# One load of ten weight rows issued as two, and waits left out that others imply, in a decode step of attention and MLP

## The chip, the cores and the metric

The kernel runs on one core of a Trainium2 chip, in one launch. The metric is the device time of one execution in microseconds (us): the kernel before takes 401.53 us, the median of 3 runs that lie between 401.38 and 401.64.

## The reference

One token passes through grouped-query attention over a cache of 65,536 positions and through a mixer with an MLP; both branches read the same normalised input and are added to it.

```python
def _A_ref(x, k_cache, v_cache, wq, wo):          # Hq = 32, Hkv = 4, Sk = 65536, Dh = 128
    q = (x @ wq).reshape(B, Sq, Hq, Dh)           # transposed to heads
    scores = jnp.einsum("bhqd,bhkd->bhqk", q, k) * (Dh ** -0.5)
    p = _softmax(scores, axis=-1)
    o = jnp.einsum("bhqk,bhkd->bhqd", p, v)
    return o.reshape(B, Sq, Hq * Dh) @ wo         # 4096 -> 1024

def _B_ref(x, w1, w2, w3, w4):                    # D = 1024, F = 3584
    h = _gelu(_layernorm(x) @ w1)
    hs = concatenate([g0, g1, g2, g3]) @ w2       # quarters of h, shifted by 1 or 2 tokens
    x1 = x + hs
    return x1 + _gelu(_layernorm(x1) @ w3) @ w4   # 3584 -> 1024

xn = _layernorm(A_x)
out = A_x + _A_ref(xn, ...) + _B_ref(xn, ...)
```

All inputs are bf16. K and V caches are 64 MB each and the weights are 42 MB together: some 170 MB are read for one row of 1,024 numbers. With one token the shifted quarters are all zero; the kernel keeps them as a tile of zeros and still multiplies it with w2.

## The kernel before, in words

**Staging.** One SBUF tile, KV, holds all large data: two slots for K (KOFF), two for V (VOFF). K comes in 16 loads of 4 MB and V in 8 loads of 8 MB; a load is issued as soon as the readers of its slot are done. All of them, and all weights, are issued by SP (`load_rows` L320, `issue_k` L334, `issue_v` L342), so they share one hardware queue, whose transfers are spread over 16 DMA engines: 8 of the 128 partitions for each engine. Every load has a semaphore of its own channel, which the 16 engines together raise by 16.

**The main loop.** There are 32 steps n, 8 for each of the 4 KV heads, each over 8,192 positions. A step transposes K on DVE (L494), forms the scores on PE (QK, L504), takes a shared bound from row maxima (stats1, MB, stats2; L511 to L521), exponentiates on ACT (L532), transposes the result through PE and DVE (L540, L542), multiplies with V on PE (PV, L550) and adds to an accumulator on POOL (FLASH, L558 to L563). Steps are written once and emitted as a loop on PE, ACT, POOL and DVE (`emit_looped`, L68): only one turn's instructions are stored, and the values of waits are computed from the turn's number (L96). SP's work isn't looped.

**The order of the work.** It is written by hand. A small planner adds the waits: each engine has a queue `_Q` with one counting semaphore, each buffer `_B` remembers which events wrote it (`w`) and read it (`r`). `_deps` (L118) makes an operation wait for the writers of what it reads and for writers and readers of what it writes. `_Q.wait` (L25) leaves a wait out when the same engine has already waited for as much on that semaphore since the last mark; each wait that is left is an instruction of its own on its engine. A full write (`set_write`) forgets earlier writers and readers, a partial one (`add_write`) does not.

**The end.** While the last steps run, SP issues w1, w2 and w3 into slots that have come free (L622 to L625), after the last step wo and the first 16 rows of w4 (L627, L628), and, when PE has read w1 and w2, the rest of w4 into their place (L652 to L658). A "row" here is 256 KB: 128 partitions with 1,024 bf16 numbers each; wo has 32 such rows, w4 has 28. The order of the queue is thus w1, w2, w3, wo, w4 rows 0 to 15, w4 rows 16 to 25, w4 rows 26 and 27.

PE's last work is, in this order: the product with w3, whose result goes through gelu into `gh_bf`; the 32 rows of wo (`half_rows`, L666); w4's first 16 rows; a small addition of the wo result into the output (L694); w4's ten rows; w4's two rows. `out_rows` (L449 to L456) does a part of w4: each row is four matmuls (L453), one for each quarter of 256 output columns, on four column groups of PE, all accumulated in the PSUM tile OUT_ps. Before each part PE waits for that part's load:

```python
w4_parts = [(0, 16, KOFF[1], b_K[1][0]), (16, 10, KOFF[0], _B()), (26, 2, KOFF[0] + 10 * D, _B())]
...
out_rows(*w4_rows(1))
out_rows(*w4_rows(2), last=True)
_op(q_dve, lambda e: e.tensor_copy(orow, OUT_ps[:, 0:256]), reads=[b_OUT], writes=[b_p[0]])
```

DVE then copies OUT_ps to bf16 (L700), SP stores 2 KB (L701) and waits for the store.

Of the kernel before, what the change touches and what calls it, by code (L numbers as in the profile page):

```python
# [13 lines left out]
class _Q:  # L14
    def __init__(self, name, sem, in_order=False):
        self.name = name
        self.sem = sem
        self.in_order = in_order
        self.ops = []
        self.cnt = 0  # L20
        self.waited = {}
        self.marks = []
        self.var = None
# [76 lines left out]
class _B:  # L100

    def __init__(self, name=""):
        self.name = name
        self.w = {}
        self.r = {}

    def set_write(self, ev):
        self.w = {ev[0]: ev[1]}
        self.r = {}

    def add_write(self, ev):
        self.w[ev[0]] = max(self.w.get(ev[0], 0), ev[1])

    def add_read(self, ev):
# [1 line left out]


def _deps(q, reads, writes):  # L118
    for b in reads:
        for s, v in b.w.items():  # L120
            q.wait((s, v))
    for b in writes:
        for s, v in list(b.w.items()) + list(b.r.items()):
            if not (q.in_order and s is q.sem):
                q.wait((s, v))


def _done(ev, reads, writes, partial=False):
# [9 lines left out]
def _op(q, fn, reads=(), writes=(), partial=False, tick=True):  # L138
    _deps(q, reads, writes)
    ev = q.op(fn, tick)  # L140
    _done(ev, reads, writes, partial)
    return ev


def _grp(q, fns, reads=(), writes=(), partial=False):
    _deps(q, reads, writes)
    ev = None
    for i, fn in enumerate(fns):
        ev = q.op(fn, i == len(fns) - 1)
    _done(ev, reads, writes, partial)  # L150
    return ev
# [8 lines left out]
def _dma(q, chan, fn, reads=(), writes=(), partial=False):  # L160
    _deps(q, reads, writes)
    chan.n += 1
    ev = q.dma(fn, chan.sem, 16 * chan.n)
    _done(ev, reads, writes, partial)
    return ev


def bass_parallel_sum__gqa_block_cached__mixer_s_mlp__decode_kernel(
# [14 lines left out]
    D = A_x.shape[2]  # L183
# [17 lines left out]
    with ExitStack() as es:  # L201
# [57 lines left out]
        KOFF, VOFF = (0, 16384), (32768, 65536)  # L259
# [39 lines left out]
        b_K = [[_B(), _B()], [_B(), _B()]]  # L299
# [149 lines left out]
        def out_rows(items, reads, last=False):  # L449
            fns = []  # L450
            for lhs, rhs in items:
                for jj in range(4):
                    fns.append(lambda e, lhs=lhs, rhs=rhs, jj=jj: e.matmul(  # L453
                        OUT_ps[32 * jj:32 * jj + 1, 0:256], lhs, rhs[:, 256 * jj:256 * jj + 256],
                        start=False, stop=last, tile_position=(0, 32 * jj), skip_group_check=True))
            _grp(q_pe, fns, reads=reads, writes=[b_OUT], partial=True)  # L456
# [192 lines left out]
        layer_norm(x1, b_x1, xn3, xn3_bf, b_xn3, 300)  # L649

        wo_sb = KV[:, VOFF[1]:VOFF[1] + 32 * D]
        w4_parts = [(0, 16, KOFF[1], b_K[1][0]), (16, 10, KOFF[0], _B()), (26, 2, KOFF[0] + 10 * D, _B())]  # L652
        for i, (r0, nr, c0, b_w) in enumerate(w4_parts):
            if i:
                for b in b_K[0]:
# [4 lines left out]
        def w4_rows(i):  # L660
            r0, nr, c0, b_w = w4_parts[i]
            return [(gh_bf[:, r:r + 1], KV[:, c0 + (r - r0) * D:c0 + (r - r0 + 1) * D]) for r in range(r0, r0 + nr)], [b_w, b_gh]
# [33 lines left out]
                                              start=False, stop=False, tile_position=(32 * (jj // 2), 32 * jj), skip_group_check=True)  # L696
                    for jj in range(4)], reads=b_ge + [b_const], writes=[b_OUT], partial=True)
        out_rows(*w4_rows(1))
        out_rows(*w4_rows(2), last=True)
        _op(q_dve, lambda e: e.tensor_copy(orow, OUT_ps[:, 0:256]), reads=[b_OUT], writes=[b_p[0]])  # L700
        ev_out = _dma(q_sp, chan("out"), lambda e: e.dma_start(out=out[0, 0, :].rearrange("(j n) -> j n", j=4), in_=orow[0:97:32, :]), reads=[b_p[0]])  # L701
        q_sp.wait(ev_out)
# [34 lines left out]
```

## Time and profile before

| what | us |
|---|---|
| median of 3 runs (lowest, highest) | 401.53 (401.38, 401.64) |
| the profiled execution | 401.81 |
| its span, from the first to the last instruction | 400.6 |
| busy: PE matmul, DVE, POOL, ACT | 167.6, 232.9, 91.8, 48.6 |
| DVE L494, transposes of K, 128 of 1.2 us | 149.5 |
| PE L504 and L550, scores and V | 60.4 and 58.6 |
| transfers of SP's queue | 169.87 MB, 98.3% of 16 engines' span |

The span is one execution, recorded by the hardware; the time of a run lies around it. Busy is the time in which an engine worked, idle the time before an instruction together with what ended it. A load is "landed" when all 16 engines have raised its semaphore. The granted clock is the share of PE's full clock that was let through.

### The profile page before, as it was taken

How to read it: one execution, taken by the hardware profiler on the slowest of the kernel's cores; microseconds unless marked ns; L12 is line 12 of the kernel's file. 1: busy time of each engine (PE TensorE's matmuls, PEld its weight loads, DVE VectorE, ACT ScalarE, POOL GpSimd, SP SyncE). 2: the span in 40 equal slices, each digit the busy share in tenths (PEclk: the TensorE clock that was granted, in tenths of full speed). 3: DMA queues.
4: the chain of work that ended last, by engine and by line, in shares of the span. 5: the costliest groups of instructions: out<-in, count | busy, mean ns of one | idle time of the engine just before them, and what ended most of it. 6: DMA issues, size and time to landing. Idle time of an engine off the chain costs nothing.

```text
span 400.6 us, 4647 instructions
## 1 busy us (share of the span) xinstructions
PE 167.6 (42%) x1488; PEld 54.5 (14%) x1504; DVE 232.9 (58%) x399; ACT 48.6 (12%) x132; POOL 91.8 (23%) x173
## 2 busy tenths in 40 slices
PE   0044233445243525352534364145335443455494
PEld 0022110111011101010111111011101110122232
DVE  0024756784688288738864886587667756643300
ACT  1000010111021101110111020111111110110000
POOL 6000013232135212230253031314232222250000
PEclk9997556555556656555555556656555555565886
DMA  9989999999999999899999998999999999999894
GB/s 393 439 373 471 414 416 422 484 398 422 458 440 406 422 474 445 389 425 468 425 409 445 474 425 386 455 442 425 429 438 461 419 422 404 474 434 459 381 425 179
DMA packets 4768, 169.98 MB, mean 424 GB/s; under 512 B 660, under 2 KB 664, under 8 KB 792
## 3 DMA queue, kind: packets, MB, share of 16 engines
q1 hardware_dynamic: 4616, 169.87, 98.3%
q8 instruction: 5, 0.08, 0.1%
q10 hardware_dynamic: 144, 0.00, 0.0%
q14 instruction: 3, 0.02, 0.0%
HBM read 169.87 MB, written 0.00 MB: 424 GB/s over the span
## 4 chain that ended last, share of the span: by engine, by line
DMA 56%; DVE 21%; PE 12%; issue 9%; another core or an unknown queue 1%; DVEq 0%; POOL 0%; ACT 0%; SPq 0%; ACTq 0%; POOLq 0%
DMA KV<-in_A_k_cache_dram 41%; DVE KV L494 16%; DMA KV<-in_B_w_dram 10%; PE S_ps L504 9%; DMA x_bf<-in_A_x_dram 6%; DVE mrow L511 2%; PE OT_ps L550 1%; PE MM_ps L465 1%; PE OUT_ps L453 1%; DVE pT_f L542 1%; PE MB_ps L517 1%; DVE Bst L521 0%; DVE Rm L512 0%; DVE brun L530 0%
## 5 line engine op out<-in xcount | busy, mean ns | idle before, releaser
L494 DVE STREAM_TRANSPOSE KV<-KV 128x1024 f32<-128x1024 f32 x128 | 149.5, 1211 | 21.8 <-DMA KV<-in_A_k_cache_dram 21.8
L504 PE MATMUL S_ps<-KV,Ycur 128*32 128x512 bf16 x512 | 60.4, 620 | 98.9 <-DVE KV L494 98.6
L550 PE MATMUL OT_ps<-KV,pT_f 128*32 128x512 bf16 x512 | 58.6, 608 | 35.2 <-DVE pT_f L542 34.4
L563 POOL TENSOR_TENSOR O_acc<-O_acc,tmpO 128x513 f32<-128x513 f32 x32 | 40.9, 1277 | 122.6 <-ACT tmpO L558 122.6
L511 DVE TENSOR_REDUCE mrow<-S_ps 128x1 f32<-128x512 f32 x32 | 22.1, 692 | 39.8 <-PE S_ps L504 39.8
L532 ACT ACTIVATE p_sb<-S_ps,brun 128x512 bf16<-128x512 f32 x32 | 22.0, 686 | 135.6 <-DVE brun L530 118.7
L558 ACT ACTIVATE tmpO<-OT_ps 128x512 f32<-128x512 f32 x32 | 19.2, 599 | 139.4 <-PE OT_ps L550 80.3
L504 PEld LDWEIGHTS S_ps<-KV,Ycur 128*32 128x32 bf16 x512 | 14.5, 126 | 123.2 <-DVE KV L494 94.2
L542 DVE STREAM_TRANSPOSE pT_f<-PT_ps 128x512 f32<-128x512 f32 x32 | 22.8, 713 | 13.5 <-PE PT_ps L540 11.0
L560 POOL TENSOR_TENSOR spare<-ff 128x1 f32<-128x1 f32 x32 | 6.2, 194 | 100.8 <-ACT ff L536 98.9
L550 PEld LDWEIGHTS OT_ps<-KV,pT_f 128*32 128x32 bf16 x512 | 15.6, 130 | 51.1 <-DVE pT_f L542 29.3
L561 POOL TENSOR_SCALAR O_acc<-O_acc,ff 128x514 f32<-128x514 f32 x32 | 22.5, 703 | 0.2 <-issue 0.2
L540 PE MATMUL PT_ps<-p_sb,permR 128*128 128x512 bf16 x16 | 8.6, 540 | 22.0 <-ACT p_sb L532 22.0
L517 PE MATMUL MB_ps<-Rm,Lmat 128*128 128x16 bf16 x32 | 6.2, 193 | 25.6 <-DVE Rm L512 25.6
L521 DVE TENSOR_REDUCE Bst<-MB_ps 128x1 f32<-128x16 f32 x32 | 5.6, 175 | 14.2 <-PE MB_ps L517 14.2
L382 PE MATMUL MM_ps<-ln_s,ones_f 128*128 128x1 f32 x6 | 1.8, 362 | 27.3 <-DVE ln_s L381 27.3
L378 DVE CAST xT<-x_bf 128x8 f32<-128x8 bf16 x1 | 0.2, 173 | 21.6 <-DMA x_bf<-in_A_x_dram 21.6
L666 PE MATMUL S_ps<-KV,o_bf 128*1 128x512 bf16 x64 | 8.8, 443 | 5.1 <-DMA KV<-in_A_wo_dram 5.1
L517 PEld LDWEIGHTS MB_ps<-Rm,Lmat 128*128 128x128 bf16 x32 | 3.3, 103 | 53.7 <-DVE Rm L512 53.7
L394 POOL TENSOR_TENSOR ln_s<-ln_s,neghalf 128x1 f32<-128x1 f32 x3 | 1.7, 560 | 37.0 <-DVE ln_s L392 37.0
L540 PEld LDWEIGHTS PT_ps<-p_sb,permR 128*128 128x128 bf16 x32 | 3.3, 102 | 47.9 <-ACT p_sb L532 47.9
L534 DVE TENSOR_TENSOR dd<-brun 128x1 f32<-128x1 f32 x32 | 5.4, 170 | 3.6
(112 smaller groups left out, 117.5 us busy)
## 6 DMA issues: line engine op xcount, KB each, us to landing
KV<-in_A_k_cache_dram SPq DMA_DIRECT2D x16, 4096.0 KB, 23.6
KV<-in_B_w_dram SPq DMA_DIRECT2D x1, 7168.0 KB, 33.0
KV<-in_B_w_dram SPq DMA_DIRECT2D x2, 2048.0 KB, 14.3
KV<-in_B_w_dram SPq DMA_DIRECT2D x1, 4096.0 KB, 34.9
KV<-in_B_w_dram SPq DMA_DIRECT2D x1, 2560.0 KB, 38.5
KV<-in_B_w_dram SPq DMA_DIRECT2D x1, 512.0 KB, 39.3
KV<-in_A_v_cache_dram SPq DMA_DIRECT2D x8, 35.9
x_bf<-in_A_x_dram ACTq DMA_DIRECT2D x1, 2.0 KB, 22.2
```

What stands on the lines that cost most here:

```text
L494: ev = q_dve.op(lambda e, c=c: e.transpose(out=KV32[:, c:c + 1024], in_=KV32[:, c:c + 1024]))
L504: fns.append(lambda e, we=we, cm=cm, mv=mv: e.matmul(S_ps[32 * cm:32 * cm + 32, :], Ycur[:, we, :, :].rearrange("p a g -> p (a g)"), mv, s ...
L511: _op(q_dve, lambda e: e.reduce_max(mrow[:, m:m + 1], S_ps[:, :], axis=AX.X), reads=[b_S], writes=[b_mrow[m]])
L517: _op(q_pe, lambda e: e.matmul(MB_ps[:, 0:16], Lmat[:, :], Rm[:, m, :], start=True, stop=True), reads=[b_R[m], b_const], writes=[b_MB])
L532: _op(q_act, lambda e: e.activation(p_sb[:, m, :], S_ps[:, :], ACTF.Exp, bias=brun[:, m:m + 1], scale=SCALE, accum_out=tmpO[:, cL:cL + 1]) ...
L540: _op(q_pe, lambda e: e.matmul(PT_ps[:, :], permR[:, :], p_sb[:, m, :], start=True, stop=True), reads=[b_p[m], b_const], writes=[b_PT])
L542: _op(q_dve, lambda e: e.transpose(out=pT_f[:, :], in_=PT_ps[:, :]), reads=[b_PT], writes=[b_pT])
L550: fns.append(lambda e, q=q, q4=q4: e.matmul(OT_ps[32 * q4:32 * q4 + 32, :], pT_bf[:, q, :, 1], KV[:, v0 + 512 * q:v0 + 512 * (q + 1)], sta ...
L558: _op(q_act, lambda e: e.activation(tmpO[:, 1:513], OT_ps[:, :], ACTF.Copy), reads=[b_OT], writes=[b_tmpO])
L561: b_Oacc.set_write(q_pool.op(lambda e: e.tensor_scalar(out=O_acc[:, :], in0=O_acc[:, :], scalar1=ff[:, m:m + 1], scalar2=0.0, op0=ALU.mult ...
L563: ev = q_pool.op(lambda e: e.tensor_tensor(out=O_acc[:, m:m + 513], in0=O_acc[:, m:m + 513], in1=tmpO[:, m:m + 513], op=ALU.add), tick=(s_ ...
L666: _grp(q_pe, [lambda e, lhs=lhs, rhs=rhs, jj=jj: e.matmul(S_ps[32 * jj:32 * jj + 1, :], lhs, rhs[:, 512 * jj:512 * jj + 512], start=False, ...
```

## The change

Two things are changed. The ten rows of w4 that follow the first sixteen are loaded as six and four, each with its own semaphore and buffer, and PE does them as two groups, each behind its own load. The places in SBUF, the order of rows and the last two rows' load are as before.

In `_deps`, waits are first gathered with the highest value for each semaphore and then issued, so an operation waits once for a semaphore where it could wait twice with a lower value first. And for a buffer whose last write was a full one and which has been read since, an operation that overwrites it waits for the readers only, since each reader has itself waited for that write. This holds for every engine, in the loops and outside.

```diff
@@ class _B
+        self.whole = False
     def set_write(self, ev):
         self.w = {ev[0]: ev[1]}
         self.r = {}
+        self.whole = True
     def add_write(self, ev):
+        self.whole = False
         self.w[ev[0]] = max(self.w.get(ev[0], 0), ev[1])
@@ def _deps(q, reads, writes):
+    need = {}
     for b in reads:
         for s, v in b.w.items():
-            q.wait((s, v))
+            need[s] = max(v, need.get(s, 0))
     for b in writes:
-        for s, v in list(b.w.items()) + list(b.r.items()):
+        for s, v in (list(b.r.items()) if b.r and b.whole else list(b.w.items()) + list(b.r.items())):
             if not (q.in_order and s is q.sem):
-                q.wait((s, v))
+                need[s] = max(v, need.get(s, 0))
+    for s, v in need.items():
+        q.wait((s, v))
@@ the end
-        w4_parts = [(0, 16, KOFF[1], b_K[1][0]), (16, 10, KOFF[0], _B()), (26, 2, KOFF[0] + 10 * D, _B())]
+        w4_parts = [(0, 16, KOFF[1], b_K[1][0]), (16, 6, KOFF[0], _B()), (22, 4, KOFF[0] + 6 * D, _B()), (26, 2, KOFF[0] + 10 * D, _B())]
...
         out_rows(*w4_rows(1))
-        out_rows(*w4_rows(2), last=True)
+        out_rows(*w4_rows(2))
+        out_rows(*w4_rows(3), last=True)
```

## The prediction

> **What bounds the kernel now.** I read the page first (engines, DMA row, queues), then the chain of waits near the end, then the windows of the last microseconds, then the timeline rows of the instructions that the change touches.
>
> The page, part 2 and part 3: the busy share of the 16 DMA engines in 40 slices of 10 us, and the queue that SP feeds.
>
> ```profile
> span 400.6 us, 4647 instructions
> ...
> DMA  9989999999999999899999998999999999999894
> ...
> q1 hardware_dynamic: 4616, 169.87, 98.3%
> ```
>
> The transfers of SP's queue fill 98.3% of the span; only the last slice (4 tenths) is not full. No engine is near that: DVE has 58%, PE 42%. So from about 2 us on, the span is 170 MB through full DMA engines, and a step counts only if it lies before the first or after the last of these bytes, or lets the queue run dry. The chain of waits, from 345 us (start, us, what):
>
> ```profile
> 357.10 38.50 DMA KV<-in_B_w_dram
> 395.59 0.04 issue
> 395.64 2.76 PE OUT_ps L453 x36
> 398.39 0.02 issue
> 398.42 0.42 DVE p_sb L700
> ```
>
> The piece of 38.50 us is the ten-row load of w4, issued at 357.10 behind everything still queued. It lands at 395.60, and only then do PE's last matmuls begin. After its landing the chain has 2.76 us of PE, 0.42 of DVE and the store. Three windows of the end (us, then PE, PEld, DVE, ACT, POOL busy with counts, granted PE clock, DMA share, GB/s):
>
> ```profile
> 390.00:394.00 4.00, 2.06 (x64) 1.16 (x56) 0.00 (x0) 0.00 (x0) 0.00 (x0) 0.99 0.98 417
> 394.00:396.00 2.00, 0.36 (x8) 0.24 (x12) 0.00 (x0) 0.00 (x0) 0.00 (x0) 0.50 0.45 176
> 396.00:397.00 1.00, 1.00 (x28) 0.69 (x20) 0.00 (x0) 0.00 (x0) 0.00 (x0) 0.50 0.04 16
> ```
>
> The DMA share falls from 0.98 to 0.45 to 0.04: the 16 engines run dry one after another over some 2 us, and the latest of them sets each landing. PE stands still from 392.06 (the end of the 391.45 row below) to 395.64, and its clock is 0.99 before and 0.50 after. PE's and SP's timeline rows, and the loads with their size and time from issue to landing:
>
> ```profile
> 389.60 1.92 PE L453 MATMUL OUT_ps<-KV,gh_bf 128*1 128x256 bf16 x64 [0.91 <-DMA KV<-in_B_w_dram]
> 391.45 0.61 PE L694 MATMUL OUT_ps<-KV,ones_f 1*1 1x256 f32 x8
> 395.64 2.73 PE L453 MATMUL OUT_ps<-KV,gh_bf 128*1 128x256 bf16 x48 [3.58 <-DMA KV<-in_B_w_dram]
> ```
>
> ```profile
> 354.65 0.36 SPq L320 DMA_DIRECT2D KV<-in_B_w_dram  x1
> 357.10 0.33 SPq L320 DMA_DIRECT2D KV<-in_B_w_dram  x1
> 357.47 0.43 SPq L320 DMA_DIRECT2D KV<-in_B_w_dram  x1
> ```
>
> ```profile
> KV<-in_B_w_dram SPq DMA_DIRECT2D x1, 4096.0 KB, 34.9
> KV<-in_B_w_dram SPq DMA_DIRECT2D x1, 2560.0 KB, 38.5
> KV<-in_B_w_dram SPq DMA_DIRECT2D x1, 512.0 KB, 39.3
> ```
>
> The three SP rows are the loads of 16, 10 and 2 rows; with the times to landing they land at 354.65 + 34.9 = 389.55, 357.10 + 38.5 = 395.60 and 357.47 + 39.3 = 396.77. The 48 matmuls of the last PE row are ten rows plus two, four matmuls a row.
>
> **The change part by part.**
>
> *The split, on SP.* One more DMA issue of 0.33 to 0.43 us. The two-row load, queued behind it on SP, is issued at about 357.9 instead of 357.47. It has 39.3 us to land and SP's next work is the store at 398.87, so this costs nothing; without that cover it would cost 0.4. The new load's waits are for the readers of w1 and w2, which the first piece has already waited for.
>
> *The split, in the DMA engines.* The bytes are the same; one more boundary between loads is passed. Ten rows take 395.60 - 389.55 = 6.05 us, 0.605 a row; two rows take 396.77 - 395.60 = 1.17, 0.585 a row. If each load cost a fixed f on top, 2r + f = 1.17 and 10r + f = 6.05 give f = -0.05, with the rounding of the landings (0.1 us) some 0.15 either way. The other end is a load with nothing queued ahead: the store, 2 KB, is issued at 398.87 and the span ends at 400.6, 1.7 us at most. So f lies between -0.2 and 1.7. I take 0.1, near the row of the same kind, a small load in a full queue. The Trainium skill, "DMA: Bandwidth & Descriptors", section "Anatomy of one DMA — SWDGE (gpsimd) path", fits about 2.0 us of fixed cost to every DMA, and most of it is the receipt after the last byte; it was measured on the other issue path. If a queue paid that for each load, the sum below would come out some 1.1 us over today's time; by the landings above, it overlaps with the next load's data.
>
> *The split, on PE.* The wait for ten rows becomes a wait for six, one for four and one for two. Six rows land four rows earlier: 395.60 - 4 x 0.605 = 393.2. The 12 rows took 2.73 us at clock 0.50; the longest matmul on this tile lasts 0.42, so a row is (2.73 - 0.42) / 11 = 0.21 us. At clock 0.99 to 1.00 the 16 rows took 1.92 with matmuls of 0.27: (1.92 - 0.27) / 15 = 0.11 a row. At the slow clock throughout:
> - six rows: 393.2 + 0.04 + 5 x 0.21 + 0.42 = 394.7, a microsecond before the next landing;
> - four rows: landing 395.60 + 0.1, + 0.04 + 3 x 0.21 + 0.42 = 396.8;
> - two rows: landing 396.77 + 0.1 = 396.87, + 0.04 + 0.21 + 0.42 = 397.54.
>
> Today PE ends at 398.39, so 0.85 us go. Next in line is the two-row load's landing; the four rows end only 0.1 before it, so a finer split would gain no more. If the clock is still 1.00, the two rows take 0.11 + 0.27 and PE ends at 397.29: 1.10 us go. Which clock holds is open: the row at 391.45 ends at 392.06, the six rows start 1.2 us later, where PE now stands for 3.58. The Trainium skill, "TensorE: Matmul & The Clock Gate", Part 1, describes a free-running window of about 3.4 us after which an idle array falls to half clock; by it the early six rows may hold the gate open, and the sum would be the 1.10. The 0.99 and 0.50 of the windows agree with two levels, and no row decides which one it will be.
>
> *DVE and the store.* L700 (0.42), the store's issue and its landing follow PE as before. Moved, not changed.
>
> *The pruned waits.* No wait is added but PE's for the new load. Behind the last landing stand three waits (PE on the load, L700 on PE, the store on L700); none has a double, so nothing goes there: the gaps are 0.04 and 0.02. In the loops, waits that others imply go, a wait being a sequencer step between instructions. The most this can free on DVE is the "issue" of a turn in the chain, 1.1 + 0.47 us, eight times over: 12.6 us of DVE. But group L494 shows 21.8 us of idle ended by the K loads: DVE already waits 2.7 us a turn for data, so it would wait longer for the same bytes. K loads are issued 23.6 us ahead of their landing (median) while 4 MB take 16 x 0.605 = 9.7, so the queue holds some 14 us of other work when one is added. Bounds: 0 from these rows; a gain would need a slice of the DMA row under 8 before the last, and there is none. I take 0. Without the cover, it would be a gain, not a loss.
>
> **Sum.** The profiled execution took 401.81 us: span 400.6 and 1.2 around it. Less 0.85 to 1.10, it gives 400.7 to 401.0. The median of the runs shown is 401.53, 0.28 under that execution, so against the runs: 400.43 to 400.68. I take 400.6.
>
> **Rivals.**
> 1. *The extra load costs what a lone one does* (slower). If the boundary stalls the queue as long as the store takes, 1.7 us, both last landings move by that: 401.53 - 0.85 - 0.1 (in the 0.85 already) + 1.7 = 402.3. It decides from f = 0.95 us on. The two-row load, a small one in the same place, speaks against it. 8%.
> 2. *A code packet moves to the latest engine.* The DMA view of 390 to 400 us has one packet of the instruction queue q8 (five of them make 0.08 MB, so 16 KB), 0.6% of 16 engines x 10 us = 0.96 us of one engine. With fewer instructions these packets fall elsewhere. On the latest engine one delays the last landing by up to 0.96: 401.5. Before, five such packets in the span and 16 engines; mostly it misses. 15%. The mirror: the latest engine is rid of one it has now, 399.7. 8%.
> 3. *It doesn't do what it says*: the six rows' last engine is so late, or PE's start of each part so slow, that PE still ends its rows in one run, and time stays at 401.5. The 2 us spread of the engines speaks for it; that each load's 16 parts follow in order on each engine, 0.6 us a row, against it. 14%.
>
> **How the numbers follow.** The forecast has 55%. A measurement here can tell about 0.2%, 0.8 us, from no change, and the forecast's low end (0.85) lies just beyond that, so I count 7 of its 55 as within. Faster: 48 + 8 = 56%; within 0.2%: 7 + 15 + 14 = 36%; slower: 8%. The range leaves out 402.3 and 399.7 (16% together): 400.2, half of the spread of the runs (0.26) and a little more under the 400.43, to 401.6.
>
> **What would show it.** After the change: PE on OUT_ps in three runs of 24, 16 and 8 matmuls, starting near 393.2, 395.7 and 396.9, each released by its own load; the idle of 3.58 us before the last run gone; L700 at about 397.3 to 397.6 instead of 398.42; the two-row load landing within 0.2 of 396.77; the DMA share of the span unchanged or higher. Wrong would be: the last landing at 397.8 or later (rivals 1 and 2), PE's last 24 matmuls in one run (rival 3), or a stretch of the loop in which the DMA share moved.

## The result, and the profile after

The changed kernel takes 400.68 us (median of 15 runs, 400.41 to 400.93), the kernel before beside it 401.55 (15 runs, 401.04 to 401.83): a ratio of 0.9979 with a 95% interval of 0.9972 to 0.9987, or 0.87 us less, between 0.5 and 1.1. The forecast was 400.6. The profiled execution of the changed kernel took 400.41 us, the lowest of its runs, that of before 401.81.

The page of the changed kernel, span and DMA row:

```profile
span 399.2 us, 4579 instructions
...
DMA  9989999999999999999999999999999999999995
```

The row is as full as before; 68 instructions fewer were recorded, and some 84 fewer ran, since the trace of before lacks 16 of PE's 1,504 matmuls. The end of the chain of waits (start, us, what; four pieces "issue" of up to 0.04 us left out):

```profile
356.89 0.33 SPq L327
357.26 0.43 SPq L327
357.74 38.81 DMA KV<-in_B_w_dram
396.55 0.04 issue
396.59 0.42 PE OUT_ps L460 x8
397.04 0.42 DVE p_sb L708
```

Before, the chain left the DMA at 395.59, with the ten rows' load, and 2.76 us of PE followed. Now it leaves it at 396.55, with the last load, and 0.42 us of PE follow. PE's three groups on the timeline (L460 is the old L453), and the times to landing of the last three loads:

```profile
392.96 0.83 PE L460 MATMUL OUT_ps<-KV,gh_bf 128*1 128x256 bf16 x24 [1.18 <-DMA KV<-in_B_w_dram]
395.39 0.61 PE L460 MATMUL OUT_ps<-KV,gh_bf 128*1 128x256 bf16 x16 [1.61 <-DMA KV<-in_B_w_dram]
396.59 0.39 PE L460 MATMUL OUT_ps<-KV,gh_bf 128*1 128x256 bf16 x8 [0.59 <-DMA KV<-in_B_w_dram]
```

```profile
KV<-in_B_w_dram SPq DMA_DIRECT2D x1, 1536.0 KB, 36.0
KV<-in_B_w_dram SPq DMA_DIRECT2D x1, 1024.0 KB, 38.1
KV<-in_B_w_dram SPq DMA_DIRECT2D x1, 512.0 KB, 38.8
```

The six, four and two rows are issued at 356.89, 357.26 and 357.74 and land at 392.89, 395.36 and, by the chain, 396.55. Each group waits for its own load and is done before the next one lands. The same windows as before (PE, PEld, DVE, ACT, POOL busy with counts, granted PE clock, DMA share, GB/s):

```profile
390.00:394.00 4.00, 2.60 (x80) 1.40 (x68) 0.00 (x0) 0.00 (x0) 0.00 (x0) 1.00 0.98 411
394.00:396.00 2.00, 0.60 (x16) 0.29 (x16) 0.00 (x0) 0.00 (x0) 0.00 (x0) 1.00 0.54 221
396.00:397.00 1.00, 0.39 (x9) 0.10 (x8) 0.00 (x0) 0.00 (x0) 0.00 (x0) 1.00 0.02 8
```

The clock is 1.00 to the end, where it was 0.50 before. From the last landing to PE's end it was 398.39 - 396.77 = 1.62 us before and is 397.01 - 396.55 = 0.46 now: 1.16 of the 1.40 us between the two profiled executions. The other 0.22 is an earlier landing, which w4's first load shows already (issued at 354.41, landed 34.9 us later, at 389.31 now; 389.55 before), so it is not the split's; in unsplit kernels PE starts on that load's rows between 389.22 and 389.73. The medians differ by 0.87 and not by 1.40 because the two profiled executions lie at opposite ends: that of before is 0.26 over the median of before, that of the changed kernel 0.27 under its own.

Two statements ahead of the prediction are to be corrected. The weights are some 36 million bytes, not 42 (170 read, less 134 for two caches of 64 times 2^20 bytes each). And not every wait is an instruction of its own: in the records most waits stand inside the instruction that needs them (353 such instructions on DVE before), and only some are a step by themselves (16 on DVE, 34 on SP).

### The profile page after: what moved, and what is told of

Same layout as the page of the kernel before. It is cut to its first block, busy times and chain, and to the rows that moved or that the text cites. A ratio compares the mean times of both kernels' runs of the same rounds, so it can differ in the third digit from the quotient of the medians.

```text
span 399.2 us, 4579 instructions
## 1 busy us (share of the span) xinstructions
PE 173.8 (44%) x1504; PEld 53.7 (13%) x1504; DVE 233.2 (58%) x399; ACT 48.8 (12%) x132; POOL 91.5 (23%) x173
## 4 chain that ended last, share of the span: by engine, by line
DMA 57%; DVE 18%; PE 13%; issue 10%; ACT 1%; another core or an unknown queue 1%; POOL 0%; DVEq 0%; SPq 0%; ACTq 0%; POOLq 0%
DMA KV<-in_A_k_cache_dram 42%; DVE KV L501 13%; DMA KV<-in_B_w_dram 10%; PE S_ps L511 9%; DMA x_bf<-in_A_x_dram 6%; DVE mrow L518 2%; PE PT_ps L547 2%; PE OT_ps L557 1%; PE MM_ps L472 1%; ACT p_sb L539 1%; DVE pT_f L549 1%; PE MB_ps L524 1%; DVE Rm L519 0%; DVE Bst L528 0%
## 5 line engine op out<-in xcount | busy, mean ns | idle before, releaser
L557 PE MATMUL OT_ps<-KV,pT_f 128*32 128x512 bf16 x512 | 57.1, 594 | 19.5 <-DVE pT_f L549 18.7
L547 PE MATMUL PT_ps<-p_sb,permR 128*128 128x512 bf16 x32 | 17.5, 547 | 44.3 <-ACT p_sb L539 44.3
## 6 DMA issues: line engine op xcount, KB each, us to landing
KV<-in_B_w_dram SPq DMA_DIRECT2D x1, 4096.0 KB, 34.9
```

What stands on the lines that cost most here:

```text
L547: _op(q_pe, lambda e: e.matmul(PT_ps[:, :], permR[:, :], p_sb[:, m, :], start=True, stop=True), reads=[b_p[m], b_const], writes=[b_PT])
L557: fns.append(lambda e, q=q, q4=q4: e.matmul(OT_ps[32 * q4:32 * q4 + 32, :], pT_bf[:, q, :, 1], KV[:, v0 + 512 * q:v0 + 512 * (q + 1)], sta ...
```

## The experiments

Two theories shared the facts. The landing theory: the end is the last landing and the rows that PE still has to do then. The clock theory: the twelve rows were late only because PE's clock had fallen to a half while it waited. A third, the wait theory, gave the gain to the pruned waits.

### The split alone

The new `w4_parts` and the fourth `out_rows`, with the old `_deps`.

> The split of the ten rows alone, with all the old waits. Landing theory (the end is the last landing plus the rows that PE still has to do then, two instead of most of twelve): 0.85 to 1.1 us under the kernel before, ratio 0.9973 to 0.9979, PE's last run 8 matmuls of 0.4 to 0.65 us. Wait theory (the pruned waits gave the gain): within 0.2 us of before.

Measured: 400.60 us against 401.59, ratio 0.9982 (0.9973 to 0.9990): as much as the whole change. The end of its chain:

```profile
396.63 0.62 PE OUT_ps L453 x8
```

Two of its windows, with the granted clock as the third figure from the end:

```profile
390.00:394.00 4.00, 2.64 (x80) 1.42 (x68) 0.00 (x0) 0.00 (x0) 0.00 (x0) 1.00 0.98 410
394.00:396.00 2.00, 0.57 (x12) 0.37 (x16) 0.00 (x0) 0.00 (x0) 0.00 (x0) 0.65 0.60 246
```

In this execution the clock had fallen again (0.65 from 394 to 396 us, 0.50 from 396 on), although the six rows had been worked on just before, so the two rows took 0.62 instead of 0.42 us. That is the prediction's case of the slow clock, with its number: 0.21 + 0.42 = 0.63. The gain is there at either clock.

### The pruned waits alone

The new `_B` and `_deps`, with ten rows in one load.

> The pruned waits alone, the ten rows in one load as before. Landing theory: within 0.2 us of before, ratio 0.9995 to 1.0005; the idle of DVE that K loads end in the transposes (21.8 us before, 23.7 in the changed kernel) is again higher than before, since DVE is freed only to wait longer. Wait theory: some 0.8 us under before.

Measured: 401.69 against 401.59, ratio 1.0004 (0.9995 to 1.0012). The wait theory falls. The transposes' group on its page (busy, mean ns | idle before, and what ended it):

```profile
L501 DVE STREAM_TRANSPOSE KV<-KV 128x1024 f32<-128x1024 f32 x128 | 149.5, 1211 | 24.2 <-DMA KV<-in_A_k_cache_dram 24.2
```

24.2 us of idle against 21.8 before. This number alone proves little: it is 22.6 with the split alone and all the old waits.

### Twelve rows in one load

```diff
-w4_parts = [(0, 16, ...), (16, 10, ...), (26, 2, ...)]
+w4_parts = [(0, 16, ...), (16, 12, ...)]
```

> The other way: the kernel before with the ten and the two rows in one load of twelve, old waits. Landing theory: all twelve rows start behind the last landing, near 396.7, and take 2.7 us at the half clock: PE ends near 399.5 instead of 398.4, 1.0 us over before, ratio 1.0025. If a load boundary in the queue cost much (rival 1 of the prediction, 1.7 us), one boundary fewer would give more than the late rows cost: 0.6 us under before.

Measured: 402.83 against 401.59, ratio 1.0038 (1.0025 to 1.0051; five runs), 1.2 us over. Its last group on PE:

```profile
396.46 2.73 PE L453 MATMUL OUT_ps<-KV,gh_bf 128*1 128x256 bf16 x48 [4.78 <-DMA KV<-in_B_w_dram]
```

All twelve rows follow the last landing, at the half clock. With the changed kernel, the kernel before and this one, 2, most of 12 and all 12 rows stand behind the last bytes, and the medians rise in that order.

### Twelve loads of one row

In the changed kernel, `w4_parts` has twelve entries of one row behind the first sixteen.

> The changed kernel with its last twelve rows in twelve loads of one row: nine boundaries more than six, four and two. By the prediction's f of 0.1 us a boundary the last landing moves by 0.9 us, and one row less behind it gives 0.1 to 0.2 back: 0.7 us over the changed kernel, near the kernel before (ratio 0.999 to 1.001). If a boundary cost nothing: 0.1 to 0.2 under the changed kernel. If it cost what the lone store takes (rival 1, 1.7 us): some 15 us over before.

Measured: 400.77 against 401.57, ratio 0.9980 (0.9971 to 0.9989): not to be told from the changed kernel, against the 0.7 us that I expected over it. Its chain's end, and three of SP's issues:

```profile
387.22 9.50 DMA KV<-in_B_w_dram
396.71 0.04 issue
396.76 0.31 PE OUT_ps L460 x4
```

```profile
359.61 4.71 SPq L327 DMA_DIRECT2D KV<-in_B_w_dram  x1
```

```profile
364.37 14.45 SPq L327 DMA_DIRECT2D KV<-in_B_w_dram  x1
```

The last landing comes 396.71 - 389.11 = 7.60 us after w4's first load, against 396.55 - 389.31 = 7.24 in the changed kernel: 0.36 us for nine boundaries, 0.04 each, by one execution of each kernel. Rival 1 of the prediction (1.7 us) is out. A row less behind the last landing gives 0.11 back (0.31 against 0.42). The SP rows come back below.

### The clock alone: extra matmuls, no split

Three kernels are the kernel before with matmuls of the same shape behind the small addition L694, written to CM_ps and read by nobody: 112, 32 and 64 of them.

```diff
+        _grp(q_pe, [lambda e, r=r, jj=jj: e.matmul(
+            CM_ps[32 * jj:32 * jj + 1, 0:256], gh_bf[:, r:r + 1], wo_sb[:, r * D + 256 * jj:r * D + 256 * jj + 256],
+            start=True, stop=True, tile_position=(0, 32 * jj), skip_group_check=True)
+            for r in range(28) for jj in range(4)], reads=[b_V[1], b_gh], writes=[b_CM])   # 8 and 16 rows in the others
         out_rows(*w4_rows(1))
```

112 extra matmuls:

> The kernel before with 112 extra matmuls of the same shape, whose result nobody reads, on PE while it would wait for the ten rows; nothing is split or pruned. The extra work takes 112 x 0.027 = 3.1 us, from 392.06 to some 395.3, before the landing at 395.6. Clock theory (the half clock of PE behind its idle of 3.58 us makes the twelve rows late): the granted clock stays at 1.00, twelve rows take 11 x 0.11 + 0.27 = 1.5 instead of 2.73 us, and since the two rows' load is there by 396.8, PE ends near 397.2: 1.1 to 1.2 us under before, as much as the split. If only the split counts (the rows are late because they start late): no more than 0.2 under before.

Measured: 401.96 against 401.59, ratio 1.0017 (1.0008 to 1.0026): slower. The chain:

```profile
392.18 1.95 PE CM_ps L698 x67
394.13 1.68 issue
395.81 1.47 PE CM_ps L698 x45
397.29 1.32 PE OUT_ps L453 x48
```

The extra work did not fit: after 67 matmuls PE stands still for 1.68 us and waits for nothing that the profile shows ("issue"); then the other 45 run when the ten rows have already landed, and push them to 397. Why PE stood still is open. That it waited for its code is a guess: in 390 to 400 us this execution has two packets of the instruction queue where before has one, but one falls between 393 and 394 us (0.93 us of one engine), the other between 396 and 397, when PE has long gone on; and the runs with 32 and 64 extra matmuls below have the additional packet too (six in the span, five before) without such an idle, though there PE waits for its load at that time. PE goes on at 395.81, just behind the landing of the ten rows (355.64 + 40.1 = 395.74), which may be chance. So this run decides nothing on the time, but its twelve rows, at a clock of 1.00, took 1.58 us instead of 2.73.

32 extra matmuls:

> The kernel before with only 32 extra matmuls (8 rows' worth, result not read) behind the small addition, so that PE reaches its wait for the ten rows at some 393.0 and does not run into code that isn't loaded yet. Clock theory: the granted clock stays at 1.00 past 395.6, the twelve rows take 1.5 to 1.6 us instead of 2.73 and PE ends near 397.2 without any split: 1.0 to 1.2 us under before. If the extra work does not hold the clock: 48 matmuls in 2.73 us as before and no gain. If PE again stands still for code in its last run, by an idle ended by issue, the gain is smaller by that idle.

Measured: 401.28 against 401.57, ratio 0.9995 (0.9986 to 1.0005), which is no verdict on a mean: of 12 executions six took 400.52 to 401.08 us and six 401.48 to 401.93. The profiled one, of 400.62 us, had the clock at 1.00:

```profile
395.59 1.60 PE L453 MATMUL OUT_ps<-KV,gh_bf 128*1 128x256 bf16 x48 [2.61 <-DMA KV<-in_B_w_dram]
```

The same 48 matmuls at 0.50 take 2.73, 1.13 us more; the two groups' medians, 400.72 and 401.73, are 1.0 apart.

64 extra matmuls:

> The kernel before, unsplit and with its old waits, with 64 extra matmuls (16 rows' worth, result not read) behind the small addition: PE works to some 393.9 and waits 1.7 us instead of 3.6. With 32 extra matmuls the executions fell into two groups, near 400.6 and near 401.7. Clock theory: the groups are the two clocks of the last twelve rows, and with 64 the full clock holds in nearly all: median 400.5 to 400.8, as low as the split, although nothing is split. If the split is needed for the gain: above 401.2, or still two groups of like size. If PE stands still for code behind the extra work: its last run starts late, by an idle ended by issue.

Measured: 400.60 us, ten of eleven executions between 400.43 and 400.96. In the profiled one the clock stays at 1.00:

```profile
395.37 1.71 PE L453 MATMUL OUT_ps<-KV,gh_bf 128*1 128x256 bf16 x48 [1.77 <-DMA KV<-in_B_w_dram]
```

The time of the split kernels, without a split. The ratio to before is only 0.9988 (0.9979 to 0.9998), because the kernel before took 401.22 in this set: six of its 15 executions lay between 400.60 and 401.00, nine between 401.21 and 401.86. So the kernel before seems to fall into the two groups too, in shares that vary: beside the changed kernel only two of its 15 executions lay under 401.2. That they are PE's two clocks is shown for the profiled executions: 0.50 at the end in those of 401.81 (before) and 401.73 (the pruned waits alone), 1.00 in 400.62 and 400.52 here. For the others it is argued from the times.

### The changed kernel with 28 extra matmuls

```diff
 out_rows(*w4_rows(1))
+_grp(q_pe, [... for r in range(7) for jj in range(4)], ..., writes=[b_CM])
 out_rows(*w4_rows(2))
```

> The changed kernel with 28 extra matmuls (result not read) between its groups of six and four rows. The clock then is 1.00 in every execution and the two rows take 0.4 us instead of 0.4 or 0.6: 0.1 to 0.25 us under the changed kernel, ratio to before 0.997 to 0.998. If the changed kernel already runs its last rows at the full clock nearly always: no difference to it.

Measured: 400.77 against 401.57, ratio 0.9980 (0.9971 to 0.9989), like the changed kernel. With two rows left, the clock is worth 0.2 us at most (0.62 against 0.42), which this measurement does not tell. No version here beats the changed kernel.

### Without the cover: six V loads left out

```diff
 def issue_v(j):
-    if j >= NV:
+    if j >= 2:
         return
```

Once in the kernel before and once in the changed one.

> The kernel before without the last six of the eight V loads (all steps multiply with the first two V blocks; the attention result is not the reference's): 50 MB fewer, so that the DMA engines no longer set the pace of the loop. Landing theory: 40 to 100 us under before, with DVE's idle for K loads gone from the transposes and the DMA share below 0.9 in the loop. If the loop's engines set the pace already: within 10 us of before.

> The changed kernel with the same six V loads left out. Here the cover of the pruned waits is gone. If the prediction's statement holds (waits cost something, but lie beside the transfers), this is 0.8 us (the split at the end) plus 1 to 12 us (waits in eight turns of the loop) under the same cut of the kernel before. If the pruned waits cost nothing at all even without cover: 0.8 us under it or less.

Measured: 381.10 us (ratio to the kernel before 0.9493, 0.9477 to 0.9509) and 380.22 (0.9472, 0.9456 to 0.9488). Neither theory's number for the first came true: it is only 20 us under before. Between 60 and 320 us the DMA share is 0.66, 1.01 before, and DVE is busy 191 of 260 us: the loop's own engines now set its pace, not far below that of the transfers. DVE's idle for K loads in the transposes is 4.1 us with the old waits, where it was 21.8. The two windows (before, then the kernel before without the six loads; columns as above):

```profile
60.00:320.00 260.00, 110.94 (x905) 30.69 (x918) 180.26 (x271) 38.47 (x109) 69.65 (x115) 0.54 1.01 435
60.00:320.00 260.00, 125.54 (x985) 33.05 (x985) 191.29 (x287) 41.91 (x117) 74.12 (x121) 0.57 0.66 274
```

The cover is some 20 us thick. The transposes of K in the two, first and last start:

```profile
L494 DVE STREAM_TRANSPOSE KV<-KV x128: 1200/1203/1246, 42.7 to 325.3; 128x1024 f32<-128x1024 f32 x128
```

```profile
L501 DVE STREAM_TRANSPOSE KV<-KV x128: 1200/1202/1245, 41.0 to 324.5; 128x1024 f32<-128x1024 f32 x128
```

282.6 us with the old waits, 283.5 with the pruned ones: the loop isn't faster where nothing hides it. The 0.88 us between the two medians (four runs each) fits what the split gives at the end: PE ends 0.6 us after the last landing in the changed kernel, 1.5 in the other.

## Why the prediction was right

**The bound.** The DMA engines full from 2 to 394 us, with only the end to be shortened: borne out (DMA share 1.00 in that stretch, before and after). The gain lies between the last landing and PE's end.

**The split on PE.** Six rows were put at 393.2, four at 395.7, two at 396.87; they landed at 392.89, 395.36 and 396.55, each some 0.3 early, 0.24 of which was there before the split. With the two rows at 0.38 us (full clock) or 0.63 (half), the measured ones are 0.42 and 0.62. The two cases of 0.85 and 1.10 us stand in the traces as split alone (0.62) and changed kernel (0.42). Two of the signs were missed by little: the last landing is 0.22 from 396.77, where 0.2 was allowed, and L700's copy starts at 397.04, ahead of the 397.3 to 397.6. The range of 400.2 to 401.6 held no gain at all as well, so it is the three groups on the timeline and not the number that bear the account out.

**The clock, weighed and left open.** That was as far as the trace of before went, but one step was missing: in the last rows of the kernel *before* the clock was taken as fixed at a half. By the times of its runs it is not. Some lie near those that end at the full clock, though no profile of such a run of this kernel was kept. At the full clock the twelve rows end about as early as the two (397.22 us with 32 extra matmuls, 397.01 in the changed kernel). Hence a second way to the whole gain, more work on PE, which the prediction's own numbers (12 rows at 0.11 us) would have priced. It also lowers the median of before, and with it the gain, where many of its executions end early: 401.22 beside the 64 extra matmuls, 401.55 beside the changed kernel.

The Trainium skill, "TensorE: Matmul & The Clock Gate", Part 1, says of its free-running window that one kernel shows a different number of slow matmuls at its start from run to run. Here it is the end that differs: the 12 runs of the kernel with 32 extra matmuls fall into two groups 1.0 us apart, which agrees if these are the two clocks. The Trainium skill, "TensorE: Matmul & The Clock Gate", Part 1, puts the fall to half clock after an idle window of about 3.4 us. Here the clock fell near 394 us, when PE had been idle for some 1.9 us (since 392.06). In the split alone it fell between 394 and 396 us although PE had been busy for 2.64 of the four microseconds before, and in the changed kernel it stayed at 1.00 to the end with 2.60 of four; the busy time alone doesn't tell the two apart.

**The boundary.** f was taken as 0.1 us with ends of -0.2 and 1.7; it is 0.04 with twelve loads and cannot be seen with three. The end of 1.7 is not paid by loads that follow one another in this full queue. The Trainium skill, "DMA: Bandwidth & Descriptors", section "Anatomy of one DMA — SWDGE (gpsimd) path", fits about 2.0 us of fixed cost to a DMA of the other issue path; the twelve loads here did not pay it one after another.

**The pruned waits.** Zero was right. The sentence that they would be a gain without cover was not: with six V loads left out, nothing came. Of the waits that are steps of their own in the records, SP's fell from 34 to 18, DVE's from 16 to 10, and PE's stayed at 9; of the instructions that hold a wait, ScalarE's fell from 211 to 163, DVE's from 353 to 346. So DVE, the busiest engine of the loop, lost almost nothing, and whether waits taken out there would have given time was not tested.

**The rivals.** Rival 1 was 40 times too dear. Rival 2 did not occur: five packets of the instruction queue before and after, at nearly the same moments. Rival 3 did not either: the three groups are apart by 1.6 and 0.6 us.

## What to carry to other kernels

Where transfers bound a kernel, look at what the consumer has left when the last bytes land, and cut the last loads so that it is little: boundaries in a full queue cost some 0.04 us here. See at which clock PE does that last work, in several executions: twelve small rows cost 1.6 or 2.7 us, depending on the clock that was granted when the wait ended, so either little work behind the last wait or a short wait before it gives the same. Waits taken out of engines that don't pace the loop gave nothing here, covered or not.

## What the runs showed of the hardware

- **A queue with many loads in it can hold the issuing engine.** With twelve small loads, SP's issues of 0.43 us grew to 4.71, 14.45 and 7.30 us, although they wait for no semaphore. When the first of them began, nine earlier loads had been issued and not yet landed; that the queue was full is inferred from this. The last load was issued at 387.22, and at 0.47 us a load it would have been at some 362 (an estimate). It was still in time, but work of SP behind it would have been held.
- **PE can stand still in a run of short matmuls, for a cause left open.** It did so for 1.68 us behind 67 matmuls that took 1.95 us together. Late code is one guess. The Trainium skill, "Runtime: NRT & Kernel Launch", section "Instruction fetch mechanics", has engines fetch code in blocks of 16 KiB over a DMA queue of their own, mostly hidden. The 16 KB packets of q8 agree with the blocks; that PE waited for one is not shown.
- **The transfers' cover was thin.** With a third fewer bytes in the loop (DMA share 0.66 where it was 1.01) the kernel took 20 us less of 401, since the loop's engines set the pace at once.
